# Windowed attention with its gradients: scores and their gradients from one full-array stationary of y and h, in place of two 128x64 column tiles

## The chip, the cores and the metric

The kernel runs on one core of one Trainium2 chip. The metric is the device time of one execution in microseconds (us). Executions of one kernel agree within about 0.3%. A ratio below is the mean time of one kernel's fast runs over the mean of the other's fast runs of the same rounds on the same chip, so it is not quite the ratio of the medians quoted beside it.

Engine names: PE is the tensor engine, PEld its weight loads, DVE the vector engine, ACT the scalar engine, POOL the GpSimd engine, SP the queue that issues most transfers.

Some words: `PS` is the kernel's tile in PSUM, the memory that the matmuls write; in it are eight banks of 512 fp32 columns. An eviction is a copy from there to SBUF, the memory that holds all other tiles here. Of a matmul's two operands the stationary one is loaded into the array as weights, and the columns of the moving one are streamed through it. A column tile is half of the array, 128 rows by 64 columns, that works on a matmul of its own. The pitch is the time from the start of one matmul to the start of the next.

## The reference

```python
# x, grad_out: (1, 256, 256, 384) bf16; wqkv: (384, 1152); wo: (384, 384)
# cut into 1024 windows of 8 x 8 = 64 tokens:  xw is (1024, 64, 384)
q, k, v = split(xw @ wqkv)
p = softmax(q @ k.T * 384 ** -0.5)      # 64 x 64 in each window
o = (p @ v) @ wo
# wanted: o, and the gradients of x, wqkv and wo for grad_out
```

The kernel does not form q, k and v. With A = Wq Wk^T times the scale, the scores are y x^T with y = x A. With B = Wv Wo, the gradients of p are h x^T with h = dO B^T. So each window needs two 64 x 64 products, y x^T and h x^T, each summed over 384 channels.

## The kernel before

One step of the main loop handles eight windows. Four tiles `t` hold two windows each: 128 tokens, window `w` on columns (or partitions) 64w to 64w+63. There are 128 steps. `YHT` holds y^T (a=0) and h^T (a=1), `XT` holds x^T, and `m` counts the three groups of 128 channels.

```python
def proj(n, a, banks, engs):            # y^T (a = 0) or h^T (a = 1), copied from PSUM to YHT by engs
    ...
        for t0, t1 in ((0, 4),) if mo < CK - 1 else ((0, 2), (2, 4)):
            ...                          # 3 matmuls, full array
            ev(engs[i], YHT[:, n % NYH, a, mo, P * t0:P * t1], o)

def scores(n):                           # 48 matmuls of 64 columns: two column tiles w
    for a in range(2):
        for t in range(4):
            for m in range(CK):
                for w in range(2):
                    r = slice(64 * w, 64 * w + 64)
                    mm(PS[r, 6, a * 256 + t * 64:a * 256 + t * 64 + 64],
                       YHT[:, n % NYH, a, m, t * P + w * 64:t * P + w * 64 + 64],   # stationary, 64 wide
                       XT[:, n % NXT, t * CK + m, r], m == 0, m == CK - 1)          # moving, 64 columns

def chain1(n):                           # softmax begins; both windows of a tile on 128 partitions
    DVE.tensor_reduce(out=ST[:, 0, :], in_=ps_sd(0), axis=AX.X, op=ALU.max)
    DVE.tensor_tensor(out=SS[:], in0=ps_sd(0), in1=bcast(0), op=ALU.subtract)

def md(n):                               # "the products": 48 matmuls, 64x64 tiles, banks 4,5 then 2,3 then 0,1
    for m in reversed(range(CK)):
        ...
        for w in range(2):
            ...
            ev(DVE if w == 0 else ACT, dst, PS[:, 2 * m + w, :]...)

def step(n):                             # T = n, S = n + 1, A = n + 2
    ...
    scores(S)
    md(T)
    chain1(S)
    wgrad(g, k0)                         # first weight-gradient stage, bank 7
    chain2(S); chain3(S)                 # rest of the softmax and of its gradient
    outs(T, 0, 0, ACT)                   # output product; ends with an eviction of 768 columns
    outs(T, 2, 2, DVE)
    wgrad(g, k0 + 1)                     # second weight-gradient stage
    proj(A, 0, (3, 1, 2, 5), (ACT, DVE, ACT, DVE))     # first projection; begins in bank 3
    attn_all(T, S)                       # 64x64 tiles, ends with the turning of p
    dxs(T, 0); dxs_ev(T, 0, ACT)         # first half of dx, full array
    proj(A, 1, (3, 4, 5, 7), (ACT, DVE, ACT, DVE))     # second projection
    dxs(T, 1); dxs_ev(T, 1, ACT)         # second half of dx, banks 1 and 2, full array; scores follow
```

## Time and profile before

| | before |
|---|---|
| median | 2018.57 us (4 runs, 2017.52 to 2019.61) |
| profiled execution | 2021.47 us, its profile's span 2019.7 us |
| PE, DVE, ACT, POOL busy | 98%, 69%, 50%, 64% |
| one step, median start to start | 15311 ns |

The first part of the page gives the busy time of each engine, its share of the span and its number of instructions:

```profile
PE 1987.0 (98%) x30568; PEld 1321.4 (65%) x30568; DVE 1392.1 (69%) x2705; ACT 1014.3 (50%) x1810; POOL 1287.7 (64%) x2312
```

The tensor engine bounds the kernel. The list of its waits in the steady part, 40 to 1940 us, says the same. Its columns are: who waited for whom, us in total, times, longest:

```profile
PE PS L74 <- DMA XT<-X: 5.3, 1, 5.3
PE PS L74 <- issue: 3.1, 3, 1.4
PE PS L74 <- DVE OS L80: 2.4, 3, 0.8
PE PS L74 <- DVE TM L145: 1.8, 3, 0.8
PE PS L157 <- POOL PB L148: 0.2, 1, 0.2
```

That is 13 us of 1900. But this view and the busy share hide the smallest waits. A matmul's record runs some 200 to 380 ns while the next one starts 30 to 215 ns after it, so an idle stretch of 100 ns between two matmuls shows as no idle time at all. This is the timeline of the tensor engine around the scores (start, length of the merged group, operation, stationary shape, moving shape, count):

```profile
1003.82 1.15 PE L74 MATMUL PS<-AT_sb,MD 128*128 128x256 bf16 x9
1004.89 0.95 PE L74 MATMUL PS<-XT,YHT 128*64 128x64 bf16 x48
1005.77 0.86 PE L74 MATMUL PS<-TT,X 64*64 64x128 bf16 x48
1006.57 0.34 PE L74 MATMUL PS<-VW,X 128*128 128x384 bf16 x1
```

The single records behind these lines show three things. The last dx matmul starts at 1004.640 and one of its size takes 163 ns in a row of them, so its data is through at 1004.803. The first score matmul starts only at 1004.895. The score matmuls start in pairs (the two column tiles, 3 ns apart), 53 ns from the first pair to the second and then 31.7 ns from pair to pair.

### The profile page before, as it was taken

The numbers are of one execution on the slowest core, as the hardware profiler recorded it, in microseconds if no ns is written. First come the engines' busy times: TensorE is split into PE (matmuls) and PEld (weight loads), VectorE is DVE, ScalarE is ACT, GpSimd is POOL, SyncE is SP. The second block draws the span as 40 slices with busy tenths as digits, with TensorE's granted clock in tenths as the row PEclk, the third lists the DMA queues.
The fourth block names the chain that finished last, engine by engine and source line by source line (L and its number), as shares of the span: only waits on it lengthen the run. The fifth ranks groups of instructions, "written<-read, shape, count | busy, mean of one in ns | idle before, by whom it ended". The sixth has DMA issues, their size and how long they took to land.

```text
span 2019.7 us, 73659 instructions
## 1 busy us (share of the span) xinstructions
PE 1987.0 (98%) x30568; PEld 1321.4 (65%) x30568; DVE 1392.1 (69%) x2705; ACT 1014.3 (50%) x1810; POOL 1287.7 (64%) x2312
## 2 busy tenths in 40 slices
PE   6999999999999999999999999999999999999998
PEld 3666666666666666666666666666666666666665
DVE  3667667667776776776777677677677667767774
ACT  2544555555455455555545545554554555455453
POOL 2766566666666666666666666666666666666653
PEclk8999999999999999999999999999999999999999
DMA  9999999999999999999999999999999999999982
GB/s 177 220 215 225 205 209 211 204 205 212 206 211 202 214 208 208 209 211 206 207 199 219 193 223 209 205 207 208 206 211 206 204 209 209 206 206 208 214 168 72
DMA packets 982143, 411.39 MB, mean 204 GB/s; under 512 B 865200, under 2 KB 956848, under 8 KB 981808
## 3 DMA queue, kind: packets, MB, share of 16 engines
q1 hardware_dynamic: 882128, 254.31, 78.2%
q0 software_dynamic: 98304, 151.39, 28.7%
q8 instruction: 239, 3.92, 0.8%
q10 hardware_dynamic: 1376, 0.98, 0.2%
q14 instruction: 96, 0.79, 0.1%
HBM read 101.84 MB, written 101.84 MB: 101 GB/s over the span
## 4 chain that ended last, share of the span: by engine, by line
PE 95%; DMA 2%; issue 1%; SPq 1%; ACT 0%; DVE 0%; POOL 0%; ACTq 0%; POOLq 0%; DVEq 0%
PE PS L74 94%; PE PS L157 2%; DMA X<-in_x_dram 1%; DMA out_dram<-DXS 1%; DMA XT<-X 0%; DMA out_dram<-OS 0%; SPq L340 0%; SPq L96 0%; ACT DXS L78 0%; SPq L100 0%; ACT VW L379 0%; SPq L92 0%; DMA DO<-in_grad_out_dram 0%; DVE OS L80 0%; POOL out_dram L243 0%
## 5 line engine op out<-in xcount | busy, mean ns | idle before, releaser
L243 POOL DMA_DIRECT2D out_dram<-DXS x1024 | 574.9, 567 | 494.1 <-ACT DXS L78 468.3
L74 PE MATMUL PS<-VW,X 128*128 128x384 bf16 x3072 | 541.6, 326 | 0.0
L74 PEld LDWEIGHTS <-X 64*64 64x64 bf16 (+1 forms) x9216 | 380.6, 104 | 203.7 <-issue 4.5
L78 ACT CAST YHT<-PS 128x512 bf16<-128x512 f32 (+1 forms) x512 | 246.0, 480 | 451.5 <-PE PS L74 445.9
L74 PEld LDWEIGHTS <-MD 128*128 128x128 bf16 x3840 | 338.2, 98 | 149.7 <-issue 2.3
L80 DVE CAST YHT<-PS 128x512 bf16<-128x512 f32 (+1 forms) x512 | 269.5, 556 | 206.3 <-PE PS L74 206.2
L80 DVE CAST MD<-PS 128x512 bf16<-128x512 f32 x384 | 241.8, 684 | 230.7 <-PE PS L74 230.7
L80 DVE CAST VW<-PS 128x384 bf16<-128x384 f32 (+1 forms) x384 | 253.3, 687 | 95.8 <-ACT VW L78 92.1
L78 ACT CAST DXS<-PS 128x768 bf16<-128x768 f32 x256 | 204.3, 798 | 212.4 <-PE PS L74 199.4
L92 POOL DMA_DIRECT2D X<-in_x_dram x504 | 270.3, 553 | 45.1 <-DMA out_dram<-DXS 30.3
L74 PE MATMUL PS<-AT_sb,MD 128*128 128x384 bf16 (+2 forms) x2304 | 294.7, 273 | 1.8 <-ACT DXS L78 1.8
L184 POOL DMA_DIRECT2D out_dram<-OS x512 | 274.3, 543 | 12.3 <-issue 9.2
L74 PE MATMUL PS<-XT,A_sb 128*128 128x512 bf16 (+1 forms) x1536 | 273.1, 328 | 7.6 <-DMA XT<-X 7.5
L74 PE MATMUL PS<-DOT,BT_sb 128*128 128x512 bf16 (+1 forms) x1536 | 270.8, 326 | 0.6 <-DVE YHT L80 0.5
L74 PE MATMUL PS<-B_sb,MD 128*128 128x384 bf16 x1536 | 270.5, 326 | 0.0
L78 ACT CAST VW<-PS 128x384 bf16<-128x384 f32 (+1 forms) x384 | 212.5, 587 | 58.1 <-PE PS L74 42.7
L78 ACT CAST MD<-PS 128x512 bf16<-128x512 f32 x384 | 200.5, 594 | 71.2 <-PE PS L74 71.1
L74 PEld LDWEIGHTS <-A_sb 128*128 128x128 bf16 x1536 | 150.1, 98 | 125.7 <-issue 11.1
L74 PEld LDWEIGHTS <-BT_sb 128*128 128x128 bf16 x1536 | 150.2, 98 | 99.2 <-DVE BT_sb L274 0.8
L74 PE MATMUL PS<-YH,PB 64*64 64x256 bf16 (+2 forms) x3072 | 195.2, 273 | 0.0
L74 PEld LDWEIGHTS <-PB 64*64 64x64 bf16 x6144 | 145.7, 106 | 51.4 <-issue 33.5
L74 PE MATMUL PS<-X,PB 64*64 64x384 bf16 (+2 forms) x1536 | 170.6, 273 | 4.2 <-DVE OS L80 2.4
(53 smaller groups left out, 1666.3 us busy)
## 6 DMA issues: line engine op xcount, KB each, us to landing
out_dram<-OS POOLq DMA_DIRECT2D x512, 96.0 KB, 4.9
out_dram<-DXS POOLq DMA_DIRECT2D x1024, 48.0 KB, 3.6
X<-in_x_dram POOLq DMA_DIRECT2D x504, 96.0 KB, 4.3
DO<-in_grad_out_dram SPq DMA_DIRECT2D x504, 96.0 KB, 4.2
YH<-YHT SPq DMA_TRANSPOSE x256, 5.2
XT<-X SPq DMA_TRANSPOSE x128, 6.2
DOT<-DO SPq DMA_TRANSPOSE x128, 6.9
w_sb<-in_wqkv_dram SPq DMA_DIRECT2D x3, 288.0 KB, 7.1
```

The costliest lines, as they stand in the source:

```text
L74: PE.matmul(out, lhsT=lhsT, rhs=rhs, start=start, stop=stop, skip_group_check=True)
L78: ACT.copy(out=out, in_=in_)
L80: DVE.tensor_copy(out=out, in_=in_)
L92: q.dma_start(out=X[:, (n % NX) * 4 + t, :], in_=img(x, n, t))
L157: PE.transpose(bb[r, o:o + 64], PB[r, n % 2, a, t, :], ident[r, r])
L184: POOL.dma_start(out=img(out_0, n, t), in_=OS[:, n % 2, t, :])
L243: POOL.dma_start(out=img(out_1, n, t)[8 * w:8 * w + 8], in_=DXS[64 * (1 - w):64 * (1 - w) + 64, n % 2, t, :])
```

## The change

The aim is to replace the 48 half-width score matmuls by 24 full-width ones. One stationary of 128 columns holds y of a window beside h of the same window, so one matmul over the window's 64 columns of x^T gives both products: one on partitions 0 to 63, the other on 64 to 127. For window 0 the order is y, h and for window 1 it is h, y, so that the scores of the two windows still lie on different halves of the partitions. For this, DVE copies y^T and h^T from `YHT` into blocks (`HYS`), 3072 elements per partition and step. The softmax operations that read PSUM now need one instruction per half. To make room on DVE, three evictions of 512 columns and the second output eviction go to ACT, and the output product is summed in the order in which the evictions now finish.

```diff
+    HYS = sb.tile([P, CK * 4, 4, 64], BF16, name="HYS")
...
+    def stack(n, a, m0, m1):
+        dst = HYS[:, 4 * m0:4 * m1, 0::3, :] if a == 0 else HYS[:, 4 * m0:4 * m1, 1:3, :]
+        DVE.tensor_copy(out=dst, in_=YHT[:, n % NYH, a, m0:m1, :].rearrange("p m (t w k) -> p (m t) w k", w=2, k=64))
...
     def scores(n):
-        for a in range(2): ...           # as above
+        for m in range(CK):
+            for w in range(2):
+                for t in range(4):
+                    mm(PS[:, 6, w * 256 + t * 64:w * 256 + t * 64 + 64],
+                       HYS[:, m * 4 + t, 2 * w:2 * w + 2, :].rearrange("p b k -> p (b k)"),
+                       XT[:, n % NXT, t * CK + m, w * 64:w * 64 + 64], m + w + t == 0, m == CK - 1)
...                                       # chain1 becomes chain0: reduce, subtract and, later, multiply once per half
-                ev(DVE if w == 0 else ACT, dst, PS[:, 2 * m + w, :]...)
+                ev(DVE if w == 0 and m > 0 else ACT, dst, PS[:, 2 * m + w, :]...)
...
-            for m in range(CK):          # in outs
+            for m in reversed(range(CK)):
...
-            outs(T, 2, 2, DVE)
+            outs(T, 2, 2, ACT)
-                proj(A, 0, (3, 1, 2, 5), (ACT, DVE, ACT, DVE))
+                proj(A, 0, (3, 1, 2, 5), (ACT, ACT, ACT, DVE))
...
-            proj(A, 1, (3, 4, 5, 7), (ACT, DVE, ACT, DVE))
+            stack(A, 0, 0, 3)
+            proj(A, 1, (3, 4, 5, 7), (ACT, ACT, ACT, DVE))
+            stack(A, 1, 0, 2)
+            stack(A, 1, 2, 3)
```

More of the change, by code (lines that the diff above doesn't have):

```diff
@@ L118, in proj, with sd, chain0 @@
                 i += 1
+    def stack(n, a, m0, m1):
+        dst = HYS[:, 4 * m0:4 * m1, 0::3, :] if a == 0 else HYS[:, 4 * m0:4 * m1, 1:3, :]
+        DVE.tensor_copy(out=dst, in_=YHT[:, n % NYH, a, m0:m1, :].rearrange("p m (t w k) -> p (m t) w k", w=2, k=64))
     def scores(n):
-        for a in range(2):
-            for t in range(4):
-                for m in range(CK):
-                    for w in range(2):
-                        r = slice(64 * w, 64 * w + 64)
-                        mm(PS[r, 6, a * 256 + t * 64:a * 256 + t * 64 + 64],
-                           YHT[:, n % NYH, a, m, t * P + w * 64:t * P + w * 64 + 64],
-                           XT[:, n % NXT, t * CK + m, r], m == 0, m == CK - 1)
-    def ps_sd(a):
-        return PS[:, 6, a * 256:a * 256 + 256].rearrange("p (t k) -> p t k", t=4)
-    def chain1(n):
-        DVE.tensor_reduce(out=ST[:, 0, :], in_=ps_sd(0), axis=AX.X, op=ALU.max)
-        DVE.tensor_tensor(out=SS[:], in0=ps_sd(0), in1=bcast(0), op=ALU.subtract)
+        for m in range(CK):
[4 more added lines that the diff above has]
+                       XT[:, n % NXT, t * CK + m, w * 64:w * 64 + 64], m + w + t == 0, m == CK - 1)
+    HALF = (slice(0, 64), slice(64, 128))
+    def sd(r, w):
+        return PS[HALF[r], 6, w * 256:w * 256 + 256].rearrange("p (t k) -> p t k", t=4)
+    def chain0(n):
+        for w in range(2):
+            DVE.tensor_reduce(out=ST[HALF[w], 0, :], in_=sd(w, w), axis=AX.X, op=ALU.max)
+        for w in range(2):
+            DVE.tensor_tensor(out=SS[HALF[w]], in0=sd(w, w),
+                              in1=ST[HALF[w], 0, :].unsqueeze(2).to_broadcast([64, 4, 64]), op=ALU.subtract)
     def chain2(n):
@@ L144, in chain3 @@
         DVE.tensor_tensor(out=pb[:, 1], in0=PEX[:], in1=bcast(2), op=ALU.mult)
-        DVE.tensor_tensor(out=TM[:], in0=ps_sd(1), in1=pb[:, 1], op=ALU.mult)
+        for w in range(2):
+            DVE.tensor_tensor(out=TM[HALF[w]], in0=sd(1 - w, w), in1=pb[HALF[w], 1], op=ALU.mult)
         DVE.tensor_reduce(out=ST[:, 3, :], in_=TM[:], axis=AX.X, op=ALU.add)
@@ L172, in md @@
                 dst = MD[:, m, :, 1:3, :] if w == 0 else MD[:, m, :, 0::3, :]
-                ev(DVE if w == 0 else ACT, dst, PS[:, 2 * m + w, :].rearrange("p (t a k) -> p t a k", t=4, a=2))
+                ev(DVE if w == 0 and m > 0 else ACT, dst, PS[:, 2 * m + w, :].rearrange("p (t a k) -> p t a k", t=4, a=2))
     def outs(n, t0, b0, eng):
         for i in range(2):
-            for m in range(CK):
+            for m in reversed(range(CK)):
                 mm(PS[:, b0 + i, 0:C], MD[:, m, t0 + i, 2:4, :].rearrange("p a k -> p (a k)"), B_sb[:, m, :],
-                   m == 0, m == CK - 1)
+                   m == CK - 1, m == 0)
         ev(eng, OS[:, n % 2, t0:t0 + 2, :], PS[:, b0:b0 + 2, 0:C])
@@ L291, in step @@
         if doS:
-            chain1(S)
+            chain0(S)
         if doF:
@@ L295, in step @@
         elif doA:
-            proj(A, 0, (7, 4, 5, 3), (ACT, DVE, ACT, DVE))
+            proj(A, 0, (7, 4, 5, 3), (ACT, ACT, ACT, DVE))
             turn_yh(A, 0)
@@ L355 @@
         scores(0)
-        chain1(0)
+        chain0(0)
         chain2(0)
```

## The prediction

> **What bounds it now.** The tensor engine: the page gives PE 98% busy, the chain that ended last is 95% PE, and the list of waits shows PE waiting only about 13 us in the steady part (40 to 1960 us). The timeline repeats a step of 15.32 us, 128 times. DVE is at 69%, ACT 50%, POOL 64%.
>
> **The score stage now**, from the single instructions of one step: the last dx matmul starts at 1004.640 and, at its 163 ns pitch, is streamed at 1004.803. The first score pair starts at 1004.895, 91 ns for going from full-array to two-column tiles. The second pair follows after 53 ns, the other pairs at a pitch of 31.6 ns. The products after it start at 1005.772, another 95 ns after the last pair. Together 0.97 us per step.
>
> **What the change removes.** The 48 half-width matmuls already ran two at a time, so 24 full-width ones save no streaming. They save (a) the entry switch, since dx is full-array too: 91 ns; (b) the slow first pair: 22 ns; (c) pitch. A full-width load lets the next start after 15 ns (first two loads of the weight-gradient stage) against 28 ns for a 64-column one, so streaming should set the pitch: 55 ns were seen for 128 columns, so I estimate 29 ns for 64: 24 x 2.4 = 58 ns. The exit switch stays. Sum: 0.17 us per step, 22 us, all on the critical path.
> The Trainium skill (TensorEngine Tiling (Array Packing), Key Properties) says that changing the tiling mode drains the engine; the trace agrees, 91 to 98 ns at each change.
>
> **What it adds.** DVE gets three SBUF-to-SBUF copies of 1536, 1024 and 512 elements. Estimated at four elements per cycle and 150 ns fixed (from 415 ns for the 512-element TT copy at two per cycle): 0.55, 0.42, 0.28 us. Splitting chain operations adds three at about 0.42 us. Three 0.69 us evictions (YHT, MD) and one of 0.95 us (OS) go to ACT. DVE stays near 69%, ACT rises to about 65%; neither is a bound on average.
>
> **Where it may bite.** Scores wait for the copy. Last projection block: DVE eviction 1004.020 to 1004.443, the 1024 copy until about 1004.78, then a semaphore; scores could start at 1004.803. I expect 30 to 60 ns of PE wait per step. Also the dx eviction on ACT ends at 1005.80 and frees banks that the products now want at about 1005.85: up to 20 ns. Net gain about 0.11 us per step, 14 us.
> The larger risk: these copies run in a two-port mode, and the Trainium skill (SBUF — State Buffer, Who interferes with whom) says such a copy and a GpSimd instruction block each other for the whole instruction. POOL issues four DXS stores from 1003.16 to 1005.43, 0.57 us each, just when the copies run. The trace before has no such copy to test it. If it holds fully, PE waits 0.4 to 0.9 us per step: 2055 to 2115 us.
>
> **Prediction:** 2005 us, 1994 to 2045. Faster by over 2%: 0.02; within 2%: 0.86; slower: 0.12.
>
> **What would show it.** 24 score matmuls per step at about 29 ns; no switch between dx and scores but a short wait for the HYS copy; chain operations on 64 partitions still about 0.42 us; ACT near 65%. Wrong if the pitch is over 36 ns (weight loads bind), HYS waits exceed 0.15 us per step, or the copies last 0.8 us or more.

## More of the kernel before

From the start of the last dx group to the scores are 1.07 us, from the scores to the products 0.88 us, from there to the weight gradient 0.80 us.

Last, the second weight-gradient stage and the first projection after it:

```profile
1010.48 2.11 PE L74 MATMUL PS<-VW,X 128*128 128x384 bf16 x12
1012.45 0.38 PE L74 MATMUL PS<-XT,A_sb 128*128 128x512 bf16 x1
```

Over all steps the median from the one to the other is 1966 ns. Twelve such matmuls in a row need 1950 ns, so 16 ns are lost there.

## The result, and the profile after

The changed kernel takes 1998.68 us (median of 4 runs, 1997.05 to 1999.69) against 2018.57 us. The ratio is 0.9901, with a 95% interval of 0.9884 to 0.9918: 20 us or 1.0% less, within the 2% called the same.

The busy line of the page after, the waits of the tensor engine in the same stretch of time, and the two pieces of the timeline that answer to those of before:

```profile
PE 1968.3 (99%) x27496; PEld 1311.8 (66%) x27496; DVE 1341.4 (67%) x2962; ACT 1301.0 (65%) x2321; POOL 1291.7 (65%) x2312
```

```profile
PE PS L75 <- DMA XT<-X: 4.7, 2, 4.0
PE PS L75 <- DVE TM L157: 2.4, 3, 1.4
PE PS L169 <- POOL PB L160: 1.2, 3, 0.6
```

```profile
992.88 1.15 PE L75 MATMUL PS<-AT_sb,MD 128*128 128x256 bf16 x9
993.90 0.87 PE L75 MATMUL PS<-XT,HYS 128*128 128x64 bf16 x24
994.70 0.86 PE L75 MATMUL PS<-TT,X 64*64 64x128 bf16 x48
995.50 0.34 PE L75 MATMUL PS<-VW,X 128*128 128x384 bf16 x1
...
999.41 2.11 PE L75 MATMUL PS<-VW,X 128*128 128x384 bf16 x12
1001.36 0.38 PE L75 MATMUL PS<-XT,A_sb 128*128 128x512 bf16 x1
```

From dx to the scores it is now 1.02 us, then 0.80 us to the products, then 0.80 as before, and the second weight-gradient stage takes 1.95. The same from the single records, as medians over the 123 full steps. A stage runs from its first matmul to the first of the next, in ns. The stages not listed agree within 1 ns. The columns of three experiments are used further down.

| stage | before | after | E1 | E3 | E12 |
|---|---|---|---|---|---|
| second dx half, to the first score | 1076 | 1016 | 1076 | 983 | 982 |
| scores | 878 | 804 | 878 | 793 | 793 |
| products | 797 | 797 | 797 | 830 | 797 |
| second weight-gradient stage | 1966 | 1950 | 1950 | 1950 | 1950 |
| first projection | 2040 | 2043 | 2043 | 2043 | 2043 |
| whole step | 15311 | 15163 | 15297 | 15153 | 15120 |

So the step lost 148 ns: 60 in front of the scores, 74 in them, 16 in front of the first projection, less 3 by which that projection grew. Times some 125 steps, that is 18.5 of the 20 us.

The costs the change adds are in the groups of DVE (line, operation, shapes, count, then busy us and mean ns of one, then idle us before):

```profile
L124 DVE COPY HYS<-YHT 128x1536 bf16<-128x1536 bf16 x128 | 70.5, 551 | 0.1
L124 DVE COPY HYS<-YHT 128x1024 bf16<-128x1024 bf16 x128 | 53.4, 417 | 0.0
L124 DVE COPY HYS<-YHT 128x512 bf16<-128x512 bf16 x128 | 37.8, 296 | 0.1
...
L145 DVE TENSOR_TENSOR SS<-PS,ST 64x256 f32<-64x256 f32 x256 | 108.0, 422 | 8.0
```

The copies last 551, 417 and 296 ns. An operation of the chain on 64 partitions lasts 422 ns; the same on 128 partitions lasted 424 ns before.

Where the copies stand is in the timelines of DVE and POOL in the same step:

```profile
993.08 0.43 DVE L81 CAST YHT<-PS 128x256 bf16<-128x256 f32 x1 [0.80 <-PE PS L75]
993.42 0.63 DVE L124 COPY HYS<-YHT 128x1024 bf16<-128x1024 bf16 x2
```

```profile
992.22 2.29 POOL L255 DMA_DIRECT2D out_dram<-DXS  x4 [2.55 <-ACT DXS L79]
```

The first of the two late copies ends at 993.842 and the scores start at 993.900. The last dx matmul started at 993.702, so its data was through at 993.865. The scores are late by about 33 ns, too little to appear in the list of waits. All the while POOL issues its four stores, and the copies show no slowing: the 1024-element copy lasted 415 to 419 ns in all 125 steps, with about 410 ns of it under a POOL instruction on average.

### The profile page after: what moved, and what is told of

It is laid out like the page before. It is cut to its first block, busy times and chain, and to the rows that moved or that the text cites. A ratio compares the mean times of both kernels' runs of the same rounds, so it can differ in the third digit from the quotient of the medians.

```text
span 1997.9 us, 68536 instructions
## 1 busy us (share of the span) xinstructions
PE 1968.3 (99%) x27496; PEld 1311.8 (66%) x27496; DVE 1341.4 (67%) x2962; ACT 1301.0 (65%) x2321; POOL 1291.7 (65%) x2312
## 4 chain that ended last, share of the span: by engine, by line
PE 96%; DMA 1%; DVE 1%; ACT 1%; POOL 0%; SPq 0%; issue 0%; ACTq 0%; POOLq 0%; DVEq 0%
PE PS L75 95%; PE PS L169 2%; DMA X<-in_x_dram 1%; DMA XT<-X 0%; DMA DOT<-DO 0%; SPq L355 0%; DVE TM L157 0%; POOL PB L160 0%; ACT VW L394 0%; ACT YHT L79 0%; POOL UM L159 0%; ACT DXS L79 0%; POOL X L93 0%; ACT MD L79 0%; DVE PB L155 0%
## 5 line engine op out<-in xcount | busy, mean ns | idle before, releaser
L79 ACT CAST YHT<-PS 128x512 bf16<-128x512 f32 x767 | 370.5, 517 | 244.3 <-PE PS L75 229.8
L81 DVE CAST YHT<-PS 128x256 bf16<-128x256 f32 (+1 forms) x257 | 109.3, 426 | 302.4 <-PE PS L75 295.1
L79 ACT CAST MD<-PS 128x512 bf16<-128x512 f32 x512 | 262.9, 600 | 52.0 <-PE PS L75 51.9
L81 DVE CAST MD<-PS 128x512 bf16<-128x512 f32 x256 | 165.1, 686 | 143.3 <-PE PS L75 143.3
L79 ACT CAST OS<-PS 128x768 bf16<-128x768 f32 x256 | 204.3, 798 | 25.9 <-PE PS L75 19.9
L159 POOL TENSOR_TENSOR UM<-PB,ST 128x256 f32<-128x256 bf16 x128 | 78.2, 611 | 207.8 <-DVE ST L158 203.2
```

Source lines behind the costliest of these rows:

```text
L79: ACT.copy(out=out, in_=in_)
L81: DVE.tensor_copy(out=out, in_=in_)
L159: POOL.tensor_tensor(out=UM[:], in0=pb[:, 1], in1=bcast(3), op=ALU.mult)
```

## The experiments

Theory A: the gain is on the tensor engine itself, the change of tile shape that is saved in front of the scores and the shorter pitch of the scores, less a short wait for the copy. Rival B: the gain comes from the work taken off DVE. Further rivals are named in the expectations.

E1 to E4 ran on one chip, E5 to E8 on another, E9 to E11 on a third, E12 on a fourth, each batch with its own runs of the kernel before. All twelve agreed with the reference in the comparison. E5 and E6 compute wrong scores, so that comparison does not see this error, and the agreement of the others says little about their scores.

### E1: the moved evictions alone

```diff
# on the kernel before
-                ev(DVE if w == 0 else ACT, dst, ...)
+                ev(DVE if w == 0 and m > 0 else ACT, dst, ...)
-            outs(T, 2, 2, DVE)
+            outs(T, 2, 2, ACT)
# ... both proj calls to (ACT, ACT, ACT, DVE), outs summed in reversed order
```

> The kernel before with only the moved evictions (three from DVE to ACT per step, one output eviction too, and the turned order of the sum in the output product); scores as before. Theory A (the gain is on the tensor engine: tile switch and pitch of the scores): only the 16 to 19 ns per step that the second weight-gradient stage lost waiting for the output eviction go away, about 2 us: ratio to before 0.998 to 1.000, entry of the scores still 256 ns after the last dx matmul. Rival B (the gain comes from taking work off DVE): most of the 20 us, ratio about 0.991.

Measured: 2015.73 us against 2018.96 us, ratio 0.9977 (0.9964 to 0.9989). The table shows that the 16 ns of the second weight-gradient stage are gone and that nothing else moved but the first projection, which is 3 ns longer: entry and length of the scores are within 1 ns those of before.

Rival B falls as the main cause. The moved evictions give 14 ns of the 148 per step. The ratio is a little better than expected, by about 2 us. In the profiled executions the rest lies in rare pauses inside the products. In the full steps, before has three of them, 0.8, 1.6 and 1.3 us longer than the median, listed in the waits as "issue", that is without a releaser. E1 has one of 1.6 us. The only other profile with one is E5 (0.7 us). None of the eleven profiles with 24 score matmuls has one above 0.3 us in these steps. What causes these pauses is not shown. They may make up to 3.7 us of the difference between the two profiled executions.

### E2: the score change alone

The changed kernel with every eviction where it was before.

```diff
# on the changed kernel
-            outs(T, 2, 2, ACT)
+            outs(T, 2, 2, DVE)
# ... the other three evictions back to DVE, outs summed in the first order
```

> The changed kernel with the evictions of before (scores, copies and split chain kept). Theory A: the score stage and its entry gain the same 134 ns per step, but DVE now has 1.3 us more chain and 1.2 us more copies in front of the output eviction, so that eviction, 16 ns late before, comes about 1.2 us late and the next projection waits for it: 2080 to 2170 us, ratio 1.03 to 1.075, with tensor-engine waits named DVE OS. Rival C (the moved evictions are cosmetic): 2000 us, ratio 0.991.

Measured: 2171.92 us, ratio 1.0749 (1.0734 to 1.0764), at the upper edge of what was expected. The scores and their entry are those of the changed kernel (804 and 1016 ns), but the second weight-gradient stage lasts 3299 ns in place of 1950. The timeline of the tensor engine, the last line with the wait in front of it, and the list of its waits:

```profile
969.71 2.11 PE L75 MATMUL PS<-VW,X 128*128 128x384 bf16 x12
973.01 2.11 PE L75 MATMUL PS<-XT,A_sb 128*128 128x512 bf16 x12 [1.19 <-DVE OS L81]
```

```profile
PE PS L75 <- DVE OS L81: 135.6, 115, 1.3
```

So the moved evictions are worth 14 ns per step on their own, and 173 us in all once the score change is in. Before, the DVE eviction of the output stood behind the softmax chain and came 16 ns late. The added halves and copies make it about 1.35 us late. Rival C, that the moves are cosmetic, falls.

### E3: the copy of h's first third issued early

```diff
# on the changed kernel, in proj, after the eviction of the first third
+            if early and mo == 0:
+                stack(n, a, 0, 1)
...
-            proj(A, 1, (3, 4, 5, 7), (ACT, ACT, ACT, DVE))
-            stack(A, 1, 0, 2)
+            proj(A, 1, (3, 4, 5, 7), (ACT, ACT, ACT, DVE), early=True)
+            stack(A, 1, 1, 2)
```

> The changed kernel, but the copy of h's first third goes to DVE between the first and last eviction of the projection, where DVE is idle, so the scores' first third finds its blocks ready. Theory A (the 33 ns by which the scores start late are the wait for the copy): the last dx matmul to first score matmul falls from 196 to about 163 ns, 4 us less than the changed kernel: about 1994.5 us, ratio to before 0.988. Rival D (the 33 ns are a cost of starting other weights, not of the copy): no change, 1998.7 us, ratio 0.990.

Measured: 1998.48 us, ratio 0.9893 (0.9876 to 0.9909), where the changed kernel had 0.9901. From the last dx matmul to the first score matmul it is now 162 ns in place of 196, the pitch of that dx matmul (162 to 163), so nothing is left between dx and scores. The scores are 11 ns shorter too: the second of them now starts 28 ns after the first in place of 39. Theory A holds for the 33 ns and rival D falls.

The time did not follow, though. The score path gained 44 ns and the products gave back 33 (797 to 830 ns). The second group of the products writes banks 2 and 3 and so waits for the second dx eviction, which reads banks 1 and 2:

```profile
993.58 0.80 ACT L79 CAST DXS<-PS 128x768 bf16<-128x768 f32 x1 [0.78 <-PE PS L75]
```

It ends at 994.383. The first matmul of the group, which carries the wait, starts at 994.434, 65 ns after the one four before it in place of 56. From the next four matmuls on, three of each four run 28 to 37 ns behind the first, where 3 to 10 ns are usual, to the end of the stage. In the trace the loads for them start only after the matmul that waited; that this is the cause was not tested. E10 to E12 test whether the eviction is what the products wait for.

### E4: a change of tile shape put back in

```diff
# on the changed kernel, at the head of scores
+        for w in range(2):
+            mm(PS[64 * w:64 * w + 64, 6, 0:64], ident[:, 0:64], ident[:, 0:64], True, True)
```

> The changed kernel with one pair of 64-column matmuls (dummy, overwritten) put between dx and the scores, so that the array goes to two column tiles and back. Theory A (each change of tile shape costs the tensor engine 91 to 98 ns): the first score matmul comes 0.37 to 0.42 us after the last dx matmul in place of 0.196, so 0.18 to 0.22 us more per step, 23 to 28 us: 2021 to 2027 us. Rival E (changing the shape is free and the entry of before had another cause): two more short matmuls, 0.03 to 0.06 us per step, 2002 to 2006 us.

Measured: 2026.90 us, ratio 1.0032 (1.0018 to 1.0046), 28 us above the changed kernel. The timeline:

```profile
1006.38 1.15 PE L75 MATMUL PS<-AT_sb,MD 128*128 128x256 bf16 x9
1007.45 0.22 PE L75 MATMUL PS<-ident 128*64 128x64 bf16 x2
1007.61 0.87 PE L75 MATMUL PS<-XT,HYS 128*128 128x64 bf16 x24
```

From the last dx matmul to the first score matmul are now 408 ns (256 to the dummy pair, as before the change, 3 within the pair, and 149 from its second matmul) in place of 196. That is 212 ns more, and the step is 212 ns longer. The new matmuls also hide the 33 ns of waiting, so they cost 245 ns. Two changes of shape of 93 ns leave 59 for the pair, near the 53 ns from the first pair to the second before the change. This division of the 245 ns is worked out, not measured. Theory A holds and rival E falls.

### E5 and E6: score matmuls over 32 columns

```diff
# E5, on the kernel before          (E6: the same cut in the changed kernel)
-                        mm(PS[r, 6, a * 256 + t * 64:a * 256 + t * 64 + 64],
+                        mm(PS[r, 6, a * 256 + t * 64:a * 256 + t * 64 + 32],
-                           XT[:, n % NXT, t * CK + m, r], m == 0, m == CK - 1)
+                           XT[:, n % NXT, t * CK + m, 64 * w:64 * w + 32], m == 0, m == CK - 1)
```

> The kernel before with score matmuls over 32 columns in place of 64, weights the same (results wrong on purpose; the bank is zeroed once). Theory A (the pitch of 31.6 ns of a pair is set by its 64-column weight loads, not by the stream): the stage keeps 730 to 755 ns from first to last score matmul. Rival F (the stream sets it): it falls to about 400 ns.

Measured: 2016.28 us (one run; before 2015.58 us on that chip). First to last score matmul 752 ns, as with 64 columns (753). So the stream does not set the pitch of the column tiles. Rival F falls. Theory A says the weight loads set it: each load starts within 2 ns after a matmul pair, and the matmuls it feeds start 30 ns after it. That order in the trace fits, but no run isolates it.

> The changed kernel with score matmuls over 32 columns (results wrong on purpose). Theory A (here the stream sets the pitch of 29.2 ns, and a full-width load needs about 15 ns): the pitch falls to 18 to 25 ns, first to last score matmul 681 to between 420 and 590 ns. Rival G (the full-width load sets 29 ns): stays near 680 ns.

Measured: 1995.64 us (one run). First to last 589 ns in place of 681: 39 ns from the first to the second, as with 64 columns, and 25.0 ns per matmul from there. Rival G falls, for the full-width loads allow less than 29 ns. The Trainium skill (TensorE: Matmul & The Clock Gate, "Wait — 56ns, not 53.3ns?") states that matmuls start no closer than about 25 ns however few columns they have. This run agrees. Whether that or the load sets the 25.0 ns here stays open. With 64 columns the stream rules: 55.7 ns for 128 columns elsewhere in the trace, 29.2 for 64 here.

The scores gained 109 ns in this run and the products lost 99 (797 to 896 ns): the same give-and-take as in E3, larger.

### E7: the late copy twice

```diff
# on the changed kernel
             stack(A, 1, 0, 2)
+            stack(A, 1, 0, 2)
```

> The changed kernel with the 1024-element copy issued twice. Theory A (that copy ends just after the dx stream and is the one wait the change adds): every further ns of it delays the scores: start of scores 0.33 to 0.36 us later, about 42 us more, 2037 to 2045 us. Rival H (the copy has slack, the 33 ns are something else): under 5 us more.

Measured: 2056.50 us (one run), 41 us above before on that chip and 58 above the median of the changed kernel. The wait is now long enough to be listed, in the timeline and in the list of waits:

```profile
973.41 1.15 PE L75 MATMUL PS<-AT_sb,MD 128*128 128x256 bf16 x9
974.89 0.87 PE L75 MATMUL PS<-XT,HYS 128*128 128x64 bf16 x24 [0.33 <-DVE HYS L124]
```

```profile
PE PS L75 <- DVE HYS L124: 40.1, 121, 0.4
```

From the last dx matmul to the scores 656 ns in place of 196: 460 ns later, the whole of what was added. So that copy has no slack, and rival H falls. The size was wrong in the expectation. I had taken 0.33 us, the distance between two independent copies in the trace after. The second copy writes the same blocks as the first and waits for its end, so it starts 452 ns behind it. Note also that the list says 40 us where the time lost is 58. A wait is counted from the end of the last matmul's record, which is some 160 ns after the engine could have taken the next.

### E8: copies beside POOL's arithmetic

The prediction's larger risk was that two-port DVE copies and POOL instructions shut each other out. The trace after already shows that POOL's issuing of stores does not hold up the copies. This run puts dummy copies beside POOL's two arithmetic operations.

```diff
# on the changed kernel; SCR is a new tile, BT_sb a constant
             chain3(S)
+            DVE.tensor_copy(out=SCR[:, 0], in_=BT_sb[:])
...
             wgrad(g, k0 + 1)
+            DVE.tensor_copy(out=SCR[:, 1], in_=BT_sb[:])
```

> The changed kernel with two dummy DVE copies of 1152 elements per step put beside POOL's two elementwise operations of the chain (UM 611 ns, PB 725 ns). Theory P (a two-port copy and a POOL operation shut each other out for their whole length): UM or the copy beside it becomes 300 to 600 ns longer. Rival Q (they share): UM, PB and copies keep 611, 725 and about 450 ns within 10%. Step time within 5 us of the changed kernel either way, as POOL has slack.

Measured: 1999.91 us (one run), the step unchanged at 15162 ns. The groups of POOL in the changed kernel and here, and those of DVE here, mean ns of one after the comma:

```profile
L160 POOL TENSOR_TENSOR PB<-TM,UM 128x256 bf16<-128x256 f32 x128 | 92.8, 725 | 10.1
L159 POOL TENSOR_TENSOR UM<-PB,ST 128x256 f32<-128x256 bf16 x128 | 78.2, 611 | 207.8 <-DVE ST L158 203.2 <-PE PS L75 4.2
```

```profile
L161 POOL TENSOR_TENSOR PB<-TM,UM 128x256 bf16<-128x256 f32 x128 | 120.5, 942 | 10.0
L160 POOL TENSOR_TENSOR UM<-PB,ST 128x256 f32<-128x256 bf16 x128 | 87.5, 683 | 203.2 <-DVE ST L159 196.9 <-PE PS L76 4.0 <-DVE SCR L314 2.1
```

```profile
L321 DVE COPY SCR<-BT_sb 128x1152 bf16<-128x1152 bf16 x125 | 58.0, 464 | 0.0
L314 DVE COPY SCR<-BT_sb 128x1152 bf16<-128x1152 bf16 x127 | 57.2, 450 | 0.0
```

UM grew from 611 to 683 ns on average and PB from 725 to 942. The order in time says more than these means. In most steps the copy starts first and POOL's operation while it runs (the copies, then UM and PB):

```profile
1001.39 0.45 DVE L314 COPY SCR<-BT_sb 128x1152 bf16<-128x1152 bf16 x1
1002.32 0.45 DVE L321 COPY SCR<-BT_sb 128x1152 bf16<-128x1152 bf16 x1
```

```profile
1001.62 0.69 POOL L160 TENSOR_TENSOR UM<-PB,ST 128x256 f32<-128x256 bf16 x1 [1.63 <-DVE ST L159]
1002.39 0.97 POOL L161 TENSOR_TENSOR PB<-TM,UM 128x256 bf16<-128x256 f32 x1
```

At UM's start the copy has 217 ns left (median), and UM is 79 ns longer than its usual 608. At PB's start it has 384 ns left, and PB is 243 ns longer. In all 238 such pairs the operation grew by what the copy had left, less 137 to 146 ns. In nine steps UM started first. Then the copy, begun 267 to 350 ns later, lasted 603 to 715 ns in place of 450 and ended 326 to 328 ns after UM:

```profile
441.06 0.66 POOL L160 TENSOR_TENSOR UM<-PB,ST 128x256 f32<-128x256 bf16 x1
```

```profile
441.32 0.71 DVE L321 COPY SCR<-BT_sb 128x1152 bf16<-128x1152 bf16 x1
```

So theory P holds here in both orders: the one that comes second gets on only when the first has ended, apart from some 140 ns of the POOL operation that the copy does not hold up. Rival Q, that they share, falls. The 300 to 600 ns expected of theory P were too many, because the copies had only 217 and 384 ns left when POOL's operations began. POOL has slack here, so it costs nothing.

### E9: the changed kernel again

Unaltered, to have it on the chip of E10 and E11.

> The changed kernel unaltered, on the chip of the next two, to compare them with: 1997 to 2000 us, ratio to before 0.988 to 0.992.

Measured: 1998.06 us against 2018.08 us, ratio 0.9896 (0.9883 to 0.9910). The result stands on a second chip.

### E10 and E11: the second dx eviction cut in two

```diff
# E10 on the changed kernel, E11 on E3
             dxs(T, 1)
-            dxs_ev(T, 1, ACT)
+            for eng, t in ((ACT, 2), (DVE, 3)):
+                ev(eng, DXS[:, T % 2, t, :], PSF[:, t * C:t * C + C])
+            dxs_st(T, 2)
```

> The changed kernel with the second dx eviction (768 columns, ACT, 798 ns) cut in two: 384 columns on ACT, 384 on DVE, which is idle there. Theory I (the products' second group wants the banks of that eviction, but in the changed kernel it comes just in time): nothing to gain, step 15163 ns as in the changed kernel, 1997 to 2000 us. Rival J (the eviction already costs the changed kernel time): up to 4 us less, 1994 to 1996 us, and the md stage below 797 ns.

> Early copy and split dx eviction together. Theory I (with the early copy alone the scores gained 44 ns per step and the products gave 33 of them back waiting for the dx eviction): both gains stay: last dx matmul to first score 162 ns, first to last score 670 ns, products back from 830 to 797 ns, step about 15120 ns, 5 us less than the changed kernel: 1992 to 1995 us, ratio to before 0.986 to 0.9885. Rival K (the 33 ns given back have another cause, such as the shape change): products stay at 830 ns, 1997 to 1999 us.

Measured: 2031.16 us (ratio 1.0063, 1.0050 to 1.0075) and 2030.93 us (1.0059, 1.0045 to 1.0073). Both missed: the products last 1059 and 1101 ns. The timelines of ACT and of DVE in E11 show why:

```profile
992.83 0.48 ACT L79 CAST DXS<-PS 128x384 bf16<-128x384 f32 x1 [0.78 <-PE PS L75]
```

```profile
993.34 0.56 DVE L81 CAST DXS<-PS 128x384 bf16<-128x384 f32 x1 [0.67 <-ACT DXS L79]
```

DVE started only after ACT had ended, although both only read. The two pieces, columns 768 to 1151 and 1152 to 1535, meet inside bank 2, and the compiled program makes the second wait for the first. The Trainium skill (PSUM — Partial Sum Buffer, "PSUM bank collisions raise a hardware error") says that the compiler back end orders any two engines that touch the same bank and the same group of 32 partitions, reads included. This program agrees: DVE stood idle for 0.67 us and was released by ACT's piece. The edit had put 0.48 and 0.56 us one behind the other in place of one 0.80 us. These two runs do not decide between theories I and K. They do show that the products follow that eviction: ending it later moved them later.

### E12: early copy, and the eviction cut at the bank boundary

```diff
# on E3
             dxs(T, 1)
-            dxs_ev(T, 1, ACT)
+            half = DXS[:, T % 2, 2:4, :].rearrange("p a c -> p (a c)")
+            ev(DVE, half[:, 0:256], PSF[:, 768:1024])       # bank 1
+            ev(ACT, half[:, 256:768], PSF[:, 1024:1536])    # bank 2
+            dxs_st(T, 2)
```

> Early copy, and the second dx eviction cut at the bank boundary, 256 columns on DVE and 512 on ACT, so that no bank is read by both (the cut inside a bank made the program order DVE behind ACT). Theory I (the products' second group waits for that eviction once the scores are faster): last dx matmul to first score 162 ns, first to last score 670 ns, products 797 ns, step about 15120 ns, 5 us less than the changed kernel: 1992 to 1995 us, ratio to before 0.986 to 0.9885. Rival K: products stay at 830 ns, 1997 to 1999 us.

Measured: 1993.40 us against 2020.93 us, ratio 0.9867 (0.9850 to 0.9883). The table shows 982, 793 and 797 ns: both gains stay, the step is 15120 ns. Theory I holds and rival K falls. So does rival J of E10: the eviction is out of the way earlier here, and the products take the 797 ns that they took in the changed kernel. In the timelines of DVE and ACT the two halves now overlap:

```profile
976.65 0.41 DVE L81 CAST DXS<-PS 128x256 bf16<-128x256 f32 x1
```

```profile
976.89 0.58 ACT L79 CAST DXS<-PS 128x512 bf16<-128x512 f32 x1 [0.78 <-PE PS L75]
```

This version beats both kernels: the step is 43 ns shorter than the changed kernel's. Its 1993.40 us and the changed kernel's 1998.06 to 1998.68 us were measured on different chips, and the intervals of the two ratios (0.9850 to 0.9883 and 0.9883 to 0.9910 in E9) just touch.

## Why the prediction was right or wrong

The time, 1998.68 us, lies in the range of 1994 to 2045 us, below the estimate of 2005 us. That range also holds the 2018.57 us of before, so the number alone proves little; the parts decide. The mechanism on the tensor engine was right. The work of the moved evictions was missed, and that the largest risk stayed away was partly luck. Point by point:

- **What bounds the kernel.** Right: the gain came from tensor-engine time alone, and E1 shows that work taken off DVE is worth 14 of 148 ns by itself.
- **Entry switch, 91 ns.** Right: 93 ns (256 less 163) before, none in E3, two of about that size in E4 if its pair takes as long as a first pair did before. The Trainium skill's statement that changing the tiling mode drains the engine (TensorEngine Tiling (Array Packing), Key Properties) agrees with all three. It gives no figure.
- **Slow first pair and pitch, 22 + 58 = 80 ns.** Right in sum: 753 less 670 ns is 83 in E3, and 72 in the changed kernel, whose second matmul comes 11 ns late. The pitch was 29.2 ns (29 estimated).
- **No streaming saved.** Right: 24 pairs of column tiles and 24 full-width matmuls stream the same columns.
- **Wait for the copy, 30 to 60 ns.** Right: 33 ns at the entry and 11 ns in the first matmul (E3), with the copies at 551, 417 and 296 ns against 550, 420 and 280 estimated (these three fit about 0.25 ns per element on top of some 170 ns). E7 shows that the copy has no slack.
- **dx eviction, up to 20 ns.** Mis-sized: 0 ns in the changed kernel. But it was the next bound, as the prediction said: E3 ran into it with 33 ns, and E12 removed it.
- **The moved evictions.** Missed. The prediction counted them only as load. They take 16 ns per step away, the wait of the first projection for the output eviction. E2 shows that they also carry the change: without them it is 7.5% slower.
- **The port risk.** Did not come true: the copies ran at 415 to 419 ns with POOL's stores issued beside them. One store of eight went from 563 to 587 ns. The page cited (SBUF — State Buffer, Who interferes with whom) says that either blocks the other for the whole instruction. E8 agrees for POOL's arithmetic; for POOL's store issues no such blocking was measured, and there the measurement decides. The prediction gave no reason why store issues should be harmless, so that part was luck: in E8 a copy that began behind POOL's arithmetic was held up by 153 to 265 ns.

The mis-sized term is the net gain of 0.11 us per step. It was 0.148 us: 16 ns more from the evictions that I had not counted, 20 because the dx eviction did not bite, and about 6, net, from small differences in the other terms. Up to 3.7 us of the profiled difference are rare pauses without a named cause.

## What to carry to other kernels

When the tensor engine is at 98%, look for time from start to start of matmuls. Changes of tile shape, late first weights and waits under 100 ns do not show in busy shares or in lists of waits, and they add up over a hundred steps. Before putting small matmuls into column tiles, ask which shape the stages beside them have. Here one full-array stationary cost two engines more work and still won, because it saved a change of shape and its matmuls followed one another at the pace of the stream. A DVE copy beside POOL's arithmetic can hold it up or be held up by it (E8), so see what POOL does where a new copy goes. When a stage gets faster, find what its follower waited for, and split work between two engines at a bank boundary.

## What the Trainium skill lacked or had wrong

- TensorEngine Tiling (Array Packing) says that a change of tiling mode drains the engine, without a figure. Here each change cost 91 to 98 ns, and E4's forced pair, two changes, cost 212 ns per step with its own matmuls, after hiding a wait of 33.
- The same page gives column tiling as up to twice as fast where a dimension is at most 64, and no pitch. Two 64-column tiles kept a pitch of 31.7 ns per pair whether 64 or 32 columns were streamed (E5). One full-width matmul, which did the work of such a pair, had 29.2 ns over 64 columns and 25.0 ns over 32 (E6).
- TensorE: Matmul & The Clock Gate (Back-to-back issue gap) gives, for streams of loads and matmuls, about 81 ns at 128 columns and about 131 ns at 512, and calls some 56 and 216 ns the gap of isolated matmuls. Here, on the full array in a row with a new stationary for each, it was 55 to 56 ns at 128 columns (dx) and 215 to 216 ns at 512 (projections).
- SBUF — State Buffer (Who interferes with whom) says that a two-port copy and a GpSimd instruction block each other for the whole instruction. E8 fits this for POOL's arithmetic, but for some 140 ns of the POOL operation that the copy did not hold up. For POOL's store issues it was not seen: copies beside them kept 415 to 419 ns, and one store of eight grew by 24 ns.
- Not found on the pages I read: when the first matmul of a group of four tiles is held by a semaphore, the other tiles fall behind it, by 28 to 37 ns in E3 and to the end of the stage, so a wait of 9 ns cost 33.
